# Keys and values of three quarters computed in the spare columns of the fourth query group

## The chip, the cores and the metric

The kernel runs on one core of one Trainium2 chip. The core has five engines that run side by side: TensorE (PE in the profile; its weight loads are PEld), VectorE (DVE), ScalarE (ACT), GpSimd (POOL) and SyncE (SP), which here only issues DMAs. The metric is the device time of one execution in microseconds, the median of several runs.

## The reference

A pre-normalized attention block with one shared key and value head, followed by a gated feed-forward block, on 2048 tokens of 448 features, all in float32:

```python
# S, D, H = 2048, 448, 16;  Dh = D // H = 28;  F = 1792
n = layernorm(x)
q = (n @ wq).reshape(B, S, H, Dh).transpose(0, 2, 1, 3)
k, v = n @ wk, n @ wv                      # one head of 28 for all 16 query heads
p = softmax(einsum("bhqd,bkd->bhqk", q, k) * Dh ** -0.5)
h = x + einsum("bhqk,bkd->bhqd", p, v).transpose(0, 2, 1, 3).reshape(B, S, H * Dh) @ wo
m = layernorm(h)
out = h + (silu(m @ w1) * (m @ w3)) @ w2
```

## The kernel before

The 2048 tokens are cut into four quarters t = 0 to 3 of 512 columns (X[t], transposed as XT[t]), the 16 heads into four groups g of four heads. A head has 28 features and lies in a band of 32 partitions, so a group fills 128 partitions and four of the 32 columns of each head's weights (WQ) are zeros. Every product with weights is made of float32 numbers split into a high and a low part: `mm_D` issues 11 matmuls, in two halves of 6 and 5.

The kernel has three parts: the front, a main loop over attention, and the feed-forward part. The change is in the front, with a tail of DMAs in the main loop. The front is an order written out by hand, the table FRONT. Each word is one step; every engine gets its instructions in the order of the words, and waits only for what an instruction needs:

- `tr.t.c`: four transposes of chunk c of quarter t (L223), and the copies to xh (ScalarE, L231) and xl (VectorE). `na`, `nm`: normalize on ScalarE, on VectorE; each is followed by a 64-column copy on GpSimd (L211). `st`: statistics on VectorE, with a power on GpSimd (L198).
- `wh`, `wp`, `wv`: split wq into high and low parts, on ScalarE, GpSimd, VectorE.
- `ka.t`, `kb.t`: the two halves of the key-value block of quarter t, 11 matmuls from WKV (wkvs). `kb` ends in the copies KH (ScalarE, L501) and vt (L503), and a DMA that doubles the 64 key rows to 128 (L504). `kl`: the low part KL on VectorE (L512), and its DMA. `va`: transposes of the values to VA.
- `kd.t`: the difference of the keys of two neighbouring quarters, on GpSimd (L507, tile kd).
- `qa.t.g`, `qb.t.g`: the two halves of the query block of quarter t and group g; `qb` ends in a copy to QR[t][:, g] (ScalarE, L534), or for group 0 of quarter 0 in the split queries qs. `qs.i`: the split of row i = 4t + g.
- `D.i.n.kp` and `U.i.n.kp`: quads, four matmuls of 32 partitions side by side (L277). A D takes scores against kd, and ScalarE applies a relu (L287); the U that follows takes them against KH, and VectorE adds both and reduces to the maximum (L291). `kp` is 0 for key quarters 0 and 1, and 1 for 2 and 3.
- `mx.0`: the row maxima of i = 0 (L307, L308) and four DMAs that put them into row 28 of qs (L314).

PSUM has eight banks of 512 columns. `bank()` deals them in the order in which `done()` gave them back, so that the table also settles which bank each step waits for.

The main loop makes 256 steps (row i, key chunk c of 128), two at a time; the units of the maxima run 20 steps ahead of it, the first 20 in the front. Work of other kinds is hung on steps by `at(step, ...)`: `max_done` and `max_out` (the max row of i, at 16i - 5 and 16i - 4), `o_norm` (DMAs sd and rb, L363 and L366), `build_qs`, and loads such as `load_w2`. What goes to SP's queue is issued strictly in that order, but as early as each DMA's own inputs allow.

Of the kernel before, what the change touches and what calls it, by code (L numbers as in the profile page):

```python
# [35 lines left out]
LAST_ORDER = ("1a 7c' 1b 4c' 6c' p0 0a 3a 1c 2a 5a 0b 2b 3b 2c 3c 5b 0c q "  # L36
              "6a 7a 5c 4a 4b 6b 7b").split()
FRONT = """
tr.0.1 tr.0.2 tr.0.3 wh.1 wh.0 ka.0 wp.0 wh.2 wp.1 st.1.1 kb.0 wh.3 wv.3 na.1.0 na.1.1 wv.2 qa.0.0
na.1.2 qa.0.1 na.1.3 st.2.1 qa.0.2 qb.0.0 qa.0.3 qb.0.2 qb.0.3 tr.1.0 tr.1.1 tr.1.2 tr.1.3 na.2.0  # L40
qb.0.1 ka.1 na.2.1 qs.2 na.2.2 kb.1 na.2.3 qa.1.0 kl.0 st.3 qa.1.2 tr.2.0 tr.2.1 tr.2.2 tr.2.3
qb.1.2 kd.1 nm.3.0 qb.1.0 nm.3.1 va.1 D.0.0.0 kl.1 qa.1.1 U.0.0.0 qb.1.1 nm.3.2 D.0.1.0 qa.1.3
nm.3.3 U.0.1.0 qb.1.3 D.0.2.0 qa.2.0 U.0.2.0 qs.1 va.0 tr.3.0 tr.3.1 tr.3.2 ka.2 tr.3.3 kb.2 kl.2
D.0.3.0 ka.3 kb.3 kl.3 kd.3 qb.2.0 U.0.3.0 qa.2.3 D.1.0.0 qb.2.3 U.1.0.0 qa.3.2 D.0.0.1 qb.3.2
U.0.0.1 qa.3.1 D.0.1.1 qb.3.1 U.0.1.1 qa.3.3 D.0.2.1 qb.3.3 U.0.2.1 qa.2.1 D.0.3.1 qb.2.1 U.0.3.1
mx.0 qa.3.0 va.3 D.1.0.1 qb.3.0 va.2 U.1.0.1 qa.2.2 qb.2.2
""".split()


# [1 line left out]
def block_kernel(  # L51
# [13 lines left out]
    ve, se, ge, pe, sy = nc.vector, nc.scalar, nc.gpsimd, nc.tensor, nc.sync  # L65
# [4 lines left out]
    def f(ap):  # L70
        return ap.bitcast(F32)
# [11 lines left out]
    ident = keep.tile([P, P], F32, name="ident")  # L83
# [3 lines left out]
    pexp, kb = small[:, :NQ], small[:64, NQ : NQ + 1]  # L87
# [3 lines left out]
    def slot(k, dt, name):  # L91
        return slots.tile([P, 2, T], dt, name=name, tag=f"slot{k}")
# [61 lines left out]
    def mm_D(ps, lhs, rhs, lsl, rsl, part=False, lows_last=False, half=None):  # L154


        terms = []
        for a, b in ((0, 0), (1, 0), (0, 1)):
            terms += [(a, c, b, c) for c in range(3)]
        terms += [(0, 3, 0, 3), (0, 3, 1, 3)][: 2 - part]  # L160
        if lows_last:
            terms.insert(6, terms.pop(9))
        for k, (a, ca, b, cb) in enumerate(terms):
            if half is None or half == (k > 5):
                pe.matmul(  # L165
                    ps, lhs[b][:, cb, lsl], rhs[a][:, ca, rsl],
                    start=(k == 0), stop=(k == len(terms) - 1 and not part),
                )
# [44 lines left out]
    XT = {}  # L213
# [35 lines left out]
    def build_qs(i, ps=None, spare=False):  # L249
        t, g = divmod(i, NG)  # L250
        QS[i] = slot(QSP[i % 3], F32R, "qs")
        MX[i] = MXS[i % 2]
        qh, ql = QS[i][:, 0], QS[i][:, 1]
        q = QR[t][:, g] if ps is None else ps
        if spare:
            ge.tensor_copy(qh, q)
        else:
            se.activation(qh, q, AF.Copy)
        (ge if ps is None else ve).tensor_tensor(ql, q, f(qh), op=ALU.subtract)
# [4 lines left out]
    def lane(j):  # L264
        return slice(32 * j, 32 * j + 32)
# [173 lines left out]
    def heat(n):  # L439
        for _ in range(n):  # L440
            pe.transpose(warm[:, :P], ident, ident)

    heat(34)
    ve.memset(VA, 1.0)
    ve.memset(f(NEG[0]), 0.0)
# [12 lines left out]

    def wq_low(eng, c):
        eng.tensor_tensor(WQ[1][:, c, :, :DH], wq4[:, c], f(WQ[0][:, c, :, :DH]), op=ALU.subtract)  # L460

    def load_wo():
        ge.memset(wo_r, 0.0)
        wov = wo.rearrange("(g j r) e -> j r g e", j=4, r=DH)
        for j in range(4):
            sy.dma_start(wo_r[32 * j : 32 * j + DH], wov[j])
# [24 lines left out]

    PP, VV = {}, {}

    def kv(half, t):
        if not half:
            PP[t] = bank()
        ps = PP[t]
        mm_D(ps[:96], WKV, XT[t], slice(0, 96), slice(0, T), half=half)
        if half:
            cols = slice(t * T, (t + 1) * T)  # L500
            se.activation(KH[0:64, cols], ps[0:64], AF.Identity, bias=kb)  # L501
            vt = VV[t] = VT[:, t % 2]
            se.activation(vt[64:96], ps[64:96], AF.Copy)  # L503
            sy.dma_start(f(KH[64:128, cols]), f(KH[0:64, cols]))  # L504

    def k_diff(t):
        ge.tensor_tensor(KD[:, t // 2], f(KH[:, t * T : (t + 1) * T]), f(KH[:, (t - 1) * T : t * T]),  # L507
                         op=ALU.subtract)

    def k_low(t):  # L510
        cols, ps = slice(t * T, (t + 1) * T), PP.pop(t)
        ve.scalar_tensor_tensor(KL[0:64, cols], ps[0:64], kb, f(KH[0:64, cols]), op0=ALU.add, op1=ALU.subtract)  # L512
        sy.dma_start(f(KL[64:128, cols]), f(KL[0:64, cols]))
        done(ps)

    def va(t):
        ps, vt = bank(), VV.pop(t)
        for n in range(NQ):
            pe.transpose(ps[:, 32 * n : 32 * n + 32], vt[64:96, n * P : (n + 1) * P], ident[64:96, 64:96])
        ve.tensor_copy(VA[:, NQ * t : NQ * t + NQ, :DH],  # L520
                       ps[:, :P].rearrange("p (n r) -> p n r", n=NQ)[:, :, :DH])
        done(ps)

    def q(half, t, g):
        if not half:
            PP[t, g] = bank()
        ps = PP[t, g]
        mm_D(ps, [w[:, :, 4 * g : 4 * g + 4].rearrange("p c h r -> p c (h r)") for w in WQ],
             XT[t], slice(0, P), slice(0, T), lows_last=True, half=half)
        if half:  # L530
            if t == g == 0:
                build_qs(0, ps)
            else:
                se.activation(QR[t][:, g], ps, AF.Copy)  # L534
            done(PP.pop((t, g)))

    def maxima(i):
# [3 lines left out]
    front = {  # L541
        "tr": ln_tr, "st": stats, "nm": ln_norm, "na": lambda t, n: ln_norm(t, n, se), "np": lambda t, n: ln_norm(t, n, ge),
        "wh": wq_high, "wp": lambda c: wq_low(ge, c), "wv": lambda c: wq_low(ve, c),
        "ka": lambda t: kv(False, t), "kb": lambda t: kv(True, t), "kl": k_low, "kd": k_diff, "va": va,
        "qa": lambda t, g: q(False, t, g), "qb": lambda t, g: q(True, t, g), "qs": build_qs,
        "D": lambda i, n, kp: quad(i, n, kp, True), "U": lambda i, n, kp: quad(i, n, kp, False), "mx": maxima,
    }
    ln_first()
    split_wkv()
# [22 lines left out]
    for i in range(NI - 1):  # L572
        e = NC * (i + 1)
# [3 lines left out]
    for t in range(NT - 1):  # L577
        e = NC * NG * (t + 1)
# [31 lines left out]
    for s in range(0, LAST, 2):  # L610
# [6 lines left out]
        for op in ORDER if us else LAST_ORDER:  # L617
# [19 lines left out]
            elif op[-1] != "'" or s != LAST - AHEAD:  # L637
                h = int(op[0])
# [64 lines left out]
    tl = NT - 1  # L703
# [83 lines left out]
```

## Time and profile before

| | us |
|---|---|
| median of 3 runs | 1180.38 (1180.21 to 1180.96) |
| the profiled execution | 1180.94 |
| its span in the trace | 1179.2 |
| first query matmul, in the span | 13.94 |
| first matmul of the main loop, in the span | 81.09 |
| first and last exponential of the main loop | 82.3 and 744.2 |

The granted clock is full in the whole span. In the rows of the timeline the first number is the start in us from the span's start, the second the length, then engine, line, operation, output and inputs, count, and in brackets the idle time before and what ended it. In a row of a table by stretch, the stretch is followed by its length, the busy time and count of PE, PEld, DVE, ACT and POOL, the clock, the DMA engines' busy share and GB/s. A row that begins with a line and has three durations gives the least, median and greatest in ns.

### The profile page before, as it was taken

To read this page: it belongs to the slowest core of one execution; us is meant where nothing else is said; L and a number is where in the kernel's file an instruction comes from. 1 tells how busy PE (TensorE), PEld (TensorE's weight loads), DVE (VectorE), ACT (ScalarE), POOL (GpSimd) and SP (SyncE) were. 2 spreads that over 40 slices of the span, in tenths; PEclk is the share of its full clock that TensorE was granted. 3 is DMA by queue.
4 is the path that set the end of the run, shared out by engine and by line. 5 is a ranking of instruction groups with operands and counts; after the bars stand their busy time and mean duration, and the time that the engine had idled before them with its cause. 6 is when DMAs were issued, how large, how long until landed. Compare 5 with 4: busy or idle time off the path is not lost. (4 is left out here: it accounts for less than half of the span.)

```text
span 1179.2 us, 24097 instructions
## 1 busy us (share of the span) xinstructions
PE 1167.5 (99%) x9585; PEld 726.4 (62%) x9585; DVE 810.8 (69%) x1478; ACT 730.9 (62%) x1389; POOL 330.2 (28%) x257
## 2 busy tenths in 40 slices
PE   9999999999999999999999999999999999999998
PEld 8654444445444445444445443688888888888887
DVE  7679999997889987999987972354454445444333
ACT  6769999996899996999986999411211111121111
POOL 4201101110110110111111032363555455455552
PEclk9999999999999999999999999999999999999999
DMA  4110101000010000010000010114000000000000
GB/s 165 32 29 2 35 16 33 12 11 2 11 45 4 11 11 2 11 47 11 3 11 11 3 46 11 42 44 118 1 32 1 1 1 32 1 1 32 1 1 32
DMA packets 32377, 26.92 MB, mean 23 GB/s; under 512 B 10824, under 2 KB 28936, under 8 KB 32264
## 3 DMA queue, kind: packets, MB, share of 16 engines
q1 hardware_dynamic: 31704, 25.32, 7.3%
q8 instruction: 75, 1.23, 0.4%
q14 instruction: 38, 0.31, 0.1%
q10 hardware_dynamic: 560, 0.06, 0.0%
HBM read 20.25 MB, written 3.80 MB: 20 GB/s over the span
## 5 line engine op out<-in xcount | busy, mean ns | idle before, releaser
L338 ACT ACTIVATE pt<-pb 128x512 f32<-128x512 f32 x1024 | 531.8, 611 | 11.6 <-PE pb L328 5.2
L283 DVE TENSOR_REDUCE mx<-pa 128x1 f32<-128x512 f32 x708 | 460.9, 684 | 52.7 <-PE pb L328 39.4
L328 PE MATMUL pb<-qs,KH 32*128 32x512 f32 x2048 | 342.7, 431 | 0.1
L277 PE MATMUL pa<-KH,qs 32*128 32x512 f32 x866 | 327.2, 488 | 0.0
L346 PE MATMUL po<-pt,VA 128*32 128x256 f32 (+1 forms) x2984 | 298.1, 471 | 5.8 <-ACT OT L350 5.4
L328 PE MATMUL pb<-qs,KL 32*128 32x512 f32 x1024 | 283.1, 419 | 0.0
L328 PEld LDWEIGHTS pb<-qs,KH 32*128 32x128 f32 x2048 | 174.6, 183 | 113.9 <-DVE mx L283 50.4
L165 PE MATMUL pa<-xh,w 128*128 128x512 f32 x784 | 202.1, 391 | 0.0
L675 ACT ACTIVATE rb<-pa 128x512 f32<-128x512 f32 x56 | 30.4, 596 | 250.5 <-PE pa L667 250.4
L165 PEld LDWEIGHTS pa<-xh,w 128*128 128x128 f32 x784 | 146.1, 188 | 30.4 <-issue 1.2
L277 PEld LDWEIGHTS pa<-KH,qs 32*128 32x128 f32 x866 | 142.3, 181 | 9.4 <-issue 2.5
L328 PEld LDWEIGHTS pb<-qs,KL 32*128 32x128 f32 x1024 | 136.6, 182 | 2.5
L692 PE MATMUL pb<-w2s,hid 128*128 128x448 f32 x648 | 136.9, 366 | 0.0
L346 PEld LDWEIGHTS po<-pt,VA 128*32 128x32 f32 x2984 | 58.8, 108 | 122.3 <-issue 105.0
L692 PEld LDWEIGHTS pb<-w2s,hid 128*128 128x128 f32 x648 | 119.4, 187 | 17.4 <-issue 9.8
L287 ACT ACTIVATE relu<-pa 128x512 f32<-128x512 f32 x158 | 91.2, 600 | 60.4 <-PE pa L277 50.1
L291 DVE CUSTOM_DVE_ANT_0 relu<-pa,relu 128x512 f32<-128x512 f32 x158 | 105.5, 682 | 9.0 <-PE pa L277 7.3
L392 POOL TENSOR_TENSOR w<-QR,w 128x1024 fp32r<-128x1024 f32 x32 | 84.0, 2640 | 92.9 <-PE pa L667 79.5
L684 DVE TENSOR_TENSOR hid<-rb,hid 128x512 fp32r<-128x512 f32 x56 | 72.6, 1296 | 39.2 <-ACT hid L683 39.2
L370 POOL TENSOR_TENSOR OT<-OT,rb 128x512 f32<-128x512 f32 x16 | 20.6, 1286 | 275.4 <-ACT pt L338 154.0
L165 PE MATMUL pa<-xl,w 128*128 128x512 f32 x336 | 94.5, 389 | 0.0
L391 DVE CAST w<-QR 128x1024 fp32r<-128x1024 f32 x32 | 22.4, 701 | 89.7 <-PE pa L165 77.3
(111 smaller groups left out, 962.3 us busy)
## 6 DMA issues: line engine op xcount, KB each, us to landing
rb<-sd SPq DMA_DIRECT2D x64, 64.0 KB
QR<-in_B_w_dram SPq DMA_DIRECT2D x16, 192.0 KB
X<-in_A_x_dram SPq DMA_DIRECT2D x3, 896.0 KB
out_dram<-X SPq DMA_DIRECT2D x3, 896.0 KB
w<-in_B_w_dram SPq DMA_DIRECT2D x8, 192.0 KB
w_wo<-in_B_w_dram SPq DMA_DIRECT2D x6, 224.0 KB
qs<-ngt SPq DMA_DIRECT2D x64, 2.0 KB
sm<-OT SPq DMA_DIRECT2D x64, 2.0 KB
```

The lines of the kernel that those rows point to most:

```text
L165: pe.matmul(ps, lhs[b][:, cb, lsl], rhs[a][:, ca, rsl], start=(k == 0), stop=(k == len(terms) - 1 and not part),)
L277: pe.matmul(self.ps, QS[i][r, 0, n * P : (n + 1) * P], ks[r], start=True, stop=True)
L283: ve.tensor_reduce(self.col(), self.ps, axis=AX.X, op=ALU.max)
L287: se.activation(r, self.ps, AF.Relu)
L291: ve.tensor_tensor_reduce(r, self.ps, r, 1.0, LOW, op0=ALU.add, op1=ALU.max, accum_out=self.col())
L328: pe.matmul(self.ps, (KH, KH, KL)[k][r, c * P : (c + 1) * P], QS[i][r, (0, 1, 0)[k]], start=(k == 0), stop=(k == 2))
L338: se.activation(pt, self.ps, AF.Exp, bias=0.0, scale=SCALE)
L346: pe.matmul(PO[i][32 * j : 32 * j + 32, q], VA[:, c], PT[i, c, j][:, q], start=(c == 0 and h0 == 0), stop=(c == NC - 1 and h1 == 2))
L392: ge.tensor_tensor(wl, W13[k], f(wh), op=ALU.subtract)
L675: se.activation(sg, ps[0], AF.Silu)
L684: ve.tensor_tensor(h[:, 1], sg, f(h[:, 0]), op=ALU.subtract)
L692: pe.matmul(Y[t][n][:, :D], hid[a][:, n * P : (n + 1) * P], w2s[:, b, :D], start=(k == 0 and m == 0), stop=(k == NF - 1 and m == 2))
```

## The change

For quarters 1 to 3 the key-value blocks are gone. The weights of group 3 are replaced by W3, whose 128 columns hold the key weights (band 0), the value weights (band 1) and heads 14 and 15 (bands 2 and 3). Heads 12 and 13, which had those bands, are cut into pieces of 12, 12 and 4 features (head 12) and 12, 8 and 8 (head 13): most go to the four unused columns of the heads of groups 0 to 2 (`wq_pads`, after the queries of quarter 0), the rest to unused columns of W3. GpSimd builds W3 with eight copies (`w3`) and the pads with eight more (`wd`). The key rows now come as 32, so that `dup` makes them 128 with three DMAs where one doubled 64. From step 18 of the main loop, `gather` collects heads 12 and 13 in rows 0 to 59 of QR[t][:, 3] with 16 DMAs a quarter, and clears the two rows that a later product must find zero. Four memsets on GpSimd are added at the start. The table FRONT is rewritten.

```diff
 FRONT = """
-tr.0.1 tr.0.2 tr.0.3 wh.1 wh.0 ka.0 wp.0 wh.2 wp.1 st.1.1 kb.0 wh.3 wv.3 na.1.0 na.1.1 wv.2 qa.0.0
...
+tr.0.1 tr.0.2 tr.0.3 wh.0 wh.1 wh.2 wp.0 wp.1 ka.0 st.1.1 wv.2 wh.3 wv.3 w3 kb.0 qa.0.1 na.1.0
...
+    W3 = slot(9, F32R, "w3")
...
+    ge.memset(f(W3.rearrange("p k (c j r) -> p k c j r", c=4, j=4)[:, :, :, 0, DH:]), 0.0)
+    for t in range(1, NT):
+        ge.memset(QR[t][0:64, 3], 0.0)
...
+    def w3_block():
+        for k in range(2):
+            w3 = W3[:, k].rearrange("p (c j r) -> p c j r", c=4, j=4)
+            ge.tensor_copy(w3[:, :, 0:2, :DH], WKV[k].rearrange("p c (j r) -> p c j r", r=32)[:, :, 0::2, :DH])
+            ge.tensor_copy(w3[:, :, 2:4, :DH], WQ[k][:, :, 14:16, :DH])
+            ge.tensor_copy(w3[:, :, 1, DH:], WQ[k][:, :, 12, 24:28])
+            ge.tensor_copy(w3[:, :, 2:4, DH:], WQ[k][:, :, 13, 20:28].rearrange("p c (j r) -> p c j r", j=2))
+
+    PADS = ((1, 12, 0, 0), (2, 12, 12, 0), (3, 13, 0, 0), (0, 13, 12, 1))
+
+    def wq_pads():
+        for k in range(2):
+            for e, h, d, g0 in PADS:
+                ge.tensor_copy(WQ[k][:, :, 4 * g0 : 12, DH + e], WQ[k][:, :, h, d : d + 12 - 4 * g0])
+
+    def gather(t, part):
+        q = QR[t]
+        if part < 4:
+            e, h, d, g0 = PADS[part]
+            r = 32 * (h - 12) + d
+            for g in range(g0, 3):
+                sy.dma_start(q[r + 4 * (g - g0) : r + 4 * (g - g0) + 4, 3], q[DH + e :: 32, g])
+        else:
+            for j in (2, 3):
+                sy.dma_start(q[44 + 4 * j : 48 + 4 * j, 3], q[32 * j + DH : 32 * j + 32, 3])
+            for g in (1, 2):
+                sy.dma_start(q[DH::32, g], q[DH:32, 3])
+            sy.dma_start(q[92::32, 3], q[DH : DH + 2, 3])
...
+    def dup(tl, n, cols):
+        for r in range(n, P, n):
+            sy.dma_start(f(tl[r : r + n, cols]), f(tl[0:n, cols]))
...
     def k_low(t):
-        cols, ps = slice(t * T, (t + 1) * T), PP.pop(t)
-        ve.scalar_tensor_tensor(KL[0:64, cols], ps[0:64], kb, f(KH[0:64, cols]), op0=ALU.add, op1=ALU.subtract)
-        sy.dma_start(f(KL[64:128, cols]), f(KL[0:64, cols]))
+        cols, ps, n = slice(t * T, (t + 1) * T), PP.pop(t), 32 if t else 64
+        ve.scalar_tensor_tensor(KL[0:n, cols], ps[0:n], kb[0:n], f(KH[0:n, cols]), op0=ALU.add, op1=ALU.subtract)
+        dup(KL, n, cols)
         done(ps)
...
-        mm_D(ps, [w[:, :, 4 * g : 4 * g + 4].rearrange("p c h r -> p c (h r)") for w in WQ],
-             XT[t], slice(0, P), slice(0, T), lows_last=True, half=half)
-        if half:
+        if t > 0 and g == 3:
+            ws = [W3[:, k].rearrange("p (c m) -> p c m", c=4) for k in range(2)]
+        else:
+            ws = [w[:, :, 4 * g : 4 * g + 4].rearrange("p c h r -> p c (h r)") for w in WQ]
+        mm_D(ps, ws, XT[t], slice(0, P), slice(0, T), lows_last=True, half=half)
+        if half and t > 0 and g == 3:
+            cols = slice(t * T, (t + 1) * T)
+            se.activation(KH[0:32, cols], ps[0:32], AF.Identity, bias=kb[0:32])
+            dup(KH, 32, cols)
+            vt = VV[t] = VT[:, t % 2]
+            se.activation(vt[32:64], ps[32:64], AF.Copy)
+            sy.dma_start(QR[t][24:28, 3], vt[60:64])
+            se.activation(QR[t][64:128, 3], ps[64:128], AF.Copy)
+            PP[t] = PP.pop((t, g))
+        elif half:
...
+    for t in range(1, NT):
+        for part in range(5):
+            at(13 + 5 * t + part, gather, t, part)
```

TensorE's rows below stand for whole steps: rows from wkvs are key-value blocks, from w_120 (W3) the new group 3, from OS_104 and OS_105 the other query blocks (high and low parts of WQ); kd is a D quad, KH a U quad, vt the transposes of `va`. First, TensorE around the keys of the last two quarters: before,

```order
L223 MATMUL pb<-ident,xn 128x128 x12
L165 MATMUL pb<-xh,wkvs 96x512 x3
L165 MATMUL pb<-xl,wkvs 96x512 x3
L223 MATMUL pb<-ident,xn 128x128 x4
L165 MATMUL pb<-xh,wkvs 96x512 x5
L277 MATMUL pa<-kd,qs 128x512 x4
L165 MATMUL pb<-xh,wkvs 96x512 x3
L165 MATMUL pb<-xl,wkvs 96x512 x3
L165 MATMUL pb<-xh,wkvs 96x512 x5
```

and in the changed kernel:

```order
L223 MATMUL pb<-ident,xn 128x128 x16
L165 MATMUL pb<-xh,w_120 128x512 x3
L165 MATMUL pb<-xl,w_120 128x512 x3
L277 MATMUL pa<-kd,qs 128x512 x4
L165 MATMUL pb<-xh,w_120 128x512 x5
L557 MATMUL pb<-ident,vt 128x32 x4
L277 MATMUL pa<-KH,qs 128x512 x4
L165 MATMUL pb<-xh,w_120 128x512 x3
L165 MATMUL pb<-xl,w_120 128x512 x3
L277 MATMUL pa<-kd,qs 128x512 x4
```

The two blocks of 11 matmuls that gave only keys and values are gone; the query blocks qa.2.3 and qa.3.3 stand in their place and are no longer among the later ones.

Second, TensorE where the quads of kp = 1 begin (U.1.0.0, then D.0.0.1 and U.0.0.1): before,

```order
L277 MATMUL pa<-KH,qs 128x512 x4
L165 MATMUL pb<-xh,OS_104 128x512 x3
L165 MATMUL pb<-xl,OS_104 128x512 x3
L277 MATMUL pa<-kd,qs 128x512 x4
L165 MATMUL pb<-xh,OS_104 128x512
L165 MATMUL pb<-xh,OS_105 128x512 x4
L277 MATMUL pa<-KH,qs 128x512 x4
```

and in the changed kernel:

```order
L277 MATMUL pa<-KH,qs 128x512 x4
L165 MATMUL pb<-xh,OS_104 128x512 x3
L165 MATMUL pb<-xl,OS_104 128x512 x3
L557 MATMUL pb<-ident,vt 128x32 x4
L277 MATMUL pa<-kd,qs 128x512 x4
L277 MATMUL pa<-KH,qs 128x512 x4
L165 MATMUL pb<-xh,OS_104 128x512
L165 MATMUL pb<-xh,OS_105 128x512 x4
```

The half query block between the D and the U is gone, and `va` has moved ahead of them; D.0.3.1, va.2 and U.0.3.1 stand together in the same way later.

Third, SP's queue in the main loop up to the max row of i = 2 (qs<-ngt): before, behind the DMAs rb of row 0,

```order
L366 DMA rb<-sd 32x512 x4
L180 DMA w2r_106<-in_B_w_dram 128x448
L180 DMA w2r_107<-in_B_w_dram 128x448
L180 DMA w2r_108<-in_B_w_dram 128x448
L314 DMA qs<-ngt_83 4x4x32 x4
```

and in the changed kernel the last part of the same stretch (QR_99 and QR_100 are quarters 2 and 3):

```order
L180 DMA w2r_106<-in_B_w_dram 128x448
L487 DMA QR_99<-QR_99 4x512 x3
L180 DMA w2r_107<-in_B_w_dram 128x448
L487 DMA QR_99<-QR_99 4x512 x2
L180 DMA w2r_108<-in_B_w_dram 128x448
L490 DMA QR_99<-QR_99 4x512 x2
L492 DMA QR_99<-QR_99 4x512 x2
L493 DMA QR_99<-QR_99 2x512
L487 DMA QR_100<-QR_100 4x512 x3
L314 DMA qs<-ngt_83 4x4x32 x4
```

Between rb and these rows stand 19 more gathers (13 of quarter 1, 6 of quarter 2), so that 32 DMAs have come between rb and the max row beside the three loads of w2.

More of the change, by code (lines that the diff above doesn't have):

```diff
@@ L38 @@
 FRONT = """
-tr.0.1 tr.0.2 tr.0.3 wh.1 wh.0 ka.0 wp.0 wh.2 wp.1 st.1.1 kb.0 wh.3 wv.3 na.1.0 na.1.1 wv.2 qa.0.0
[L40 to L46, printed above, removed]
+tr.0.1 tr.0.2 tr.0.3 wh.0 wh.1 wh.2 wp.0 wp.1 ka.0 st.1.1 wv.2 wh.3 wv.3 w3 kb.0 qa.0.1 na.1.0
+qa.0.0 na.1.1 qa.0.2 na.1.2 qa.0.3 na.1.3 st.2 kl.0 qb.0.0 qb.0.2 tr.1.0 tr.1.1 tr.1.2 tr.1.3 qb.0.1
+qa.1.3 qb.0.3 wd qb.1.3 nm.2.0 nm.2.1 nm.2.2 nm.2.3 st.3 kl.1 tr.2.0 qa.1.2 tr.2.1 kd.1 tr.2.2
+qb.1.2 tr.2.3 qa.1.0 va.0 D.0.0.0 nm.3.0 qb.1.0 qs.1 nm.3.1 nm.3.2 U.0.0.0 qa.1.1 D.0.1.0 qb.1.1
+nm.3.3 U.0.1.0 tr.3.0 tr.3.1 tr.3.2 tr.3.3 qa.2.3 D.0.2.0 qb.2.3 va.1 U.0.2.0 qa.3.3 D.0.3.0 qb.3.3
+kl.2 U.0.3.0 qa.2.2 D.1.0.0 qb.2.2 kl.3 U.1.0.0 qa.2.0 va.3 kd.3 D.0.0.1 U.0.0.1 qb.2.0 D.0.1.1
+qa.3.1 U.0.1.1 qb.3.1 D.0.2.1 qa.3.2 U.0.2.1 qb.3.2 D.0.3.1 va.2 U.0.3.1 mx.0 qs.2 qa.2.1 D.1.0.1
+qb.2.1 U.1.0.1 qa.3.0 qb.3.0
 """.split()
@@ L503, in kv @@
             se.activation(vt[64:96], ps[64:96], AF.Copy)
-            sy.dma_start(f(KH[64:128, cols]), f(KH[0:64, cols]))
+            dup(KH, 64, cols)
     def k_diff(t):
@@ L517, in va @@
         ps, vt = bank(), VV.pop(t)
+        r = lane(1 if t else 2)
         for n in range(NQ):
-            pe.transpose(ps[:, 32 * n : 32 * n + 32], vt[64:96, n * P : (n + 1) * P], ident[64:96, 64:96])
+            pe.transpose(ps[:, 32 * n : 32 * n + 32], vt[r, n * P : (n + 1) * P], ident[r, r])
         ve.tensor_copy(VA[:, NQ * t : NQ * t + NQ, :DH],
@@ L545, in block_kernel @@
         "qa": lambda t, g: q(False, t, g), "qb": lambda t, g: q(True, t, g), "qs": build_qs,
-        "D": lambda i, n, kp: quad(i, n, kp, True), "U": lambda i, n, kp: quad(i, n, kp, False), "mx": maxima,
+        "D": lambda i, n, kp: quad(i, n, kp, True), "U": lambda i, n, kp: quad(i, n, kp, False), "mx": maxima, "w3": w3_block, "wd": wq_pads,
     }
```

## Prediction

> **What bounds the kernel now.** I read the page's busy line first, then a table of engine busy time by stretch, then TensorE's own waits in the first 90 us, then the timeline of the front, which is the only part that the change writes anew.
>
> ```profile
> PE 1167.5 (99%) x9585; PEld 726.4 (62%) x9585; DVE 810.8 (69%) x1478; ACT 730.9 (62%) x1389; POOL 330.2 (28%) x257
> 13.94:81.09 67.15, 67.15 (x354) 46.64 (x352) 48.84 (x135) 46.71 (x86) 15.34 (x26) 1.00 0.11 32
> PE pb L441 <- POOL small L416: 1.3, 1, 1.3
> ```
>
> The second row is the stretch from the first matmul of the queries (13.94 us) to the first of the main loop (81.09 us): TensorE is busy in all 67.15 us at full clock, VectorE in 48.84, ScalarE in 46.71, GpSimd in 15.34. The third is the only wait of TensorE that the trace names up to 90 us, and it lies at the start. So the front is bounded by TensorE's own issue, and matmuls taken out there are worth their issue time until another engine's chain becomes late. Since busy time of pipelined matmuls is modelled, I price them by distances between starts:
>
> ```profile
> 13.94 0.85 PE L165 MATMUL pb<-xh,OS 128*128 128x512 f32 x3
> 17.36 0.84 PE L165 MATMUL pb<-xl,OS 128*128 128x512 f32 x3
> 25.70 0.85 PE L165 MATMUL pb<-xh,wkvs 128*96 128x512 f32 x3
> 28.26 0.85 PE L165 MATMUL pb<-xh,OS 128*128 128x512 f32 x3
> 54.48 0.51 PE L277 MATMUL pa<-KH,qs 32*128 32x512 f32 x4
> 54.92 0.95 PE L165 MATMUL pb<-xh,OS 128*128 128x512 f32 x3
> 56.50 0.50 PE L277 MATMUL pa<-kd,qs 32*128 32x512 f32 x4
> 56.93 1.43 PE L165 MATMUL pb<-xh,OS 128*128 128x512 f32 x5
> 58.29 0.51 PE L277 MATMUL pa<-KH,qs 32*128 32x512 f32 x4
> 75.66 0.25 PE L519 MATMUL pb<-ident,vt 32*128 32x32 f32 x1
> 76.34 1.44 PE L165 MATMUL pb<-xh,OS 128*128 128x512 f32 x5
> ```
>
> Rows one and two: 15 matmuls in 3.42 us, 0.228 each. Rows three and four: one whole key-value block (11 matmuls) is 2.56 us. Rows five to nine: a period of two quads (D, U) and one query block (11 matmuls) is 58.29 - 54.48 = 3.81 us; less 11 x 0.228 = 2.51, a quad between full-height matmuls costs 0.65: 0.22 to get in, 0.22 for its four parallel matmuls, 0.22 to get out. The last two rows: va and a quad together take 0.68 where a quad takes 0.44, so an adjacent va costs 0.24.
>
> **The change, part by part.**
>
> *Removed.* Three key-value blocks (quarters 2 to 4): 3 x 2.56 = 7.7 us of TensorE. On ScalarE nothing goes: KH, vt and QR of group 3 are still copied, the last with 64 rows at the same width. Four normalizations move from ScalarE to VectorE (nm.2 for na.2), about 2 us on an engine with 18 us free.
>
> *Order.* D.0.0.1 with U.0.0.1, and D.0.3.1 with va.2 and U.0.3.1, stand next to one another: each pair saves one way out and one way in, 2 x 0.44 = 0.9 us. TensorE's floor is therefore 8.6 us under before. Against it stand three waits, which I find by walking the new order with the row prices (query half 1.37 or 1.14 us, quad 0.65).
>
> *Wait 1, kd.3 (the difference of key quarters 3 and 2).*
>
> ```profile
> 53.53 0.68 ACT L501 ACTIVATE KH<-pb,small 64x512 fp32r<-64x512 f32 x1
> 54.24 0.46 SPq L504 DMA_DIRECT2D KH<-KH  x1
> 56.95 1.32 POOL L507 TENSOR_TENSOR kd<-KH 128x512 fp32r<-128x512 f32 x1 [9.41 <-DMA KH<-KH]
> 57.03 2.07 ACT L287 ACTIVATE relu<-pa 128x512 f32<-128x512 f32 x4 [1.58 <-PE pa L277]
> 58.93 0.69 DVE L291 CUSTOM_DVE_ANT_0 relu<-pa,relu 128x512 f32<-128x512 f32 x1 [0.89 <-PE pa L277]
> 59.55 0.69 DVE L291 CUSTOM_DVE_ANT_0 relu<-pa,relu 128x512 f32<-128x512 f32 x1
> 135.30 1.72 SPq L366 DMA_DIRECT2D rb<-sd  x4
> 138.97 1.28 POOL L370 TENSOR_TENSOR OT<-OT,rb 128x512 f32<-128x512 f32 x1 [16.40 <-ACT pt L338]
> ```
>
> From the start of the copy on ScalarE to the DMA is 0.71 us, from one DMA to kd 2.71, kd itself 1.32. Now three DMAs of 32 rows follow one another. The rb rows show four such DMAs, 0.43 apart, all landed 2.4 us after the last began; so the third costs 2 x 0.45 more, bounded by 0 and by 2 x 2.71. In the walk qb.3.3 ends at 49.7, but ScalarE is in the relus of D.0.3.0 until 50.8 (0.53 behind its quad, 0.52 each). KH.3 starts there, DMAs at 51.5, 52.0, 52.4, data at 54.9, kd.3 done at 56.2. TensorE reaches D.0.0.1 at 55.9 plus 0.2 for a bank of the relus of D.1.0.0. With a handover it waits 0.3 to 0.5. kd.1 in the same way: DMAs from 29.2, done near 34.1, wanted at 34.4: no wait, by 0.3 us.
>
> *Waits 2 and 3, PSUM banks of the adjacent quads.* The eight banks are dealt in the order in which they come free. One is held by the open query block and one went through va.3, so the fourth matmul of U.0.0.1 gets the bank that the first relu of D.0.0.1 leaves: 0.53 + 0.52 + 0.1 = 1.1 us after that quad started, where it would have come 0.22 after. That is 0.9 lost. U.0.3.1 gets the last two banks of U.0.2.1, whose reductions (first 0.64 behind its quad, 0.61 each) end 3.1 us after it started, so 1.3 after D.0.3.1 began (0.44 + 1.14 + 0.22 lie between); with va.2 it would have come 0.5 after. With the handover 0.9 is lost again, 1.8 together: the adjacency gives more back than it saves.
>
> *Loop start.*
>
> ```profile
> 73.62 0.51 PE L277 MATMUL pa<-KH,qs 32*128 32x512 f32 x4
> 76.83 0.22 DVE L307 TENSOR_REDUCE neg<-mx 128x16 fp32r<-128x64 f32 x1
> 77.36 2.44 SPq L314 DMA_DIRECT2D qs<-ngt  x4
> 81.09 0.50 PE L277 MATMUL pa<-KH,qs 32*128 32x512 f32 x1
> 81.38 0.46 PE L328 MATMUL pb<-qs,KH 32*128 32x512 f32 x1
> ```
>
> From U.0.3.1 (73.62) to the max row's DMAs is 3.74 us and from these to the first score matmul (81.38) 4.02, which bounds how long the four DMAs take. After U.0.3.1 the new order has two query blocks and two quads, 6.3 us and a 0.2 way in, against 7.47 before: it lacks two va. Since U.0.3.1 waits as above, its DMAs go out near 71.6, and the score matmul can follow by 75.6; TensorE arrives at 75.5 to 75.8. Wait at most 0.1. The six KL copies ahead of them on SP go out behind kl.3, by 57.
>
> *Sum.* -7.7 - 0.9 + 0.4 (kd.3) + 0.3 (single banks of the relus around U.1.0.0) + 1.8 (waits 2, 3) + 0.1 = -6.0; the walk itself, with a few hundredths at each handover, sets the loop's start at 75.5 against 81.09, -5.6. I take -5.7.
>
> *Costed at nothing: GpSimd.*
>
> ```profile
> 58.20 1.60 POOL L463 MEMSET OT<- 128x1792 f32 x1
> 4.66 0.57 POOL L198 TENSOR_TENSOR rs<-rs,small 128x1 f32<-128x1 f32 x1 [2.93 <-DVE rs L197]
> 18.22 0.25 POOL L201 TENSOR_SCALAR rs<-rs 128x4 f32<-128x4 f32 x1
> L256 POOL CAST qs<-QR 128x512 fp32r<-128x512 f32 x13 | 7.9, 611 | 246.7 <-PE pb L328 246.7
> L211 POOL COPY xn<-xn 128x64 f32<-128x64 f32 x32 | 9.2, 297 | 16.6 <-DVE xn L209 6.5 <-ACT xn L207 6.5 <-PE pb L519 2.4
> ```
>
> The new memsets (three of 512 columns, 1.60 x 512/1792 = 0.46 each, one small) lie in the 2.93 us before 4.66. The eight copies of w3 have 16 to 224 elements: between 0.2 and 0.4 by the last two rows, 2.3 us together, or 4.9 if each took the whole 0.61. They start at 18.5 and stand ahead of the xn copies that tr.1.3 wants at 23.1: free up to about 3.6 us (4 x 0.27 for the xn copies behind them), 1.3 lost at the upper end. The lower end is taken, as the sizes lie around the 64-column row. The eight pad copies (48 elements) start behind qb.0.3's first matmul at 26.3, 0.25 each, done by 28.4; qa.1.2 wants the first four at 28.8 and qb.1.2 the rest at 31.1.
>
> *Costed at nothing: the 48 gather DMAs on SP's queue.* They run in the main loop, where the groups that they complete are built from step 49 on. But SP issues in order, and the max row of unit row i = 2 stands behind 32 of them.
>
> ```profile
> L504 SPq DMA_DIRECT2D KH<-KH x4: 461/475/509, 14.9 to 54.2; - x4
> L366 SPq DMA_DIRECT2D rb<-sd x64: 307/413/1653, 135.3 to 766.4; - x64
> L355 SPq DMA_DIRECT2D sm<-OT x64: 513/588/1706, 125.7 to 748.7; - x64
> 137.07 1.37 SPq L180 DMA_DIRECT2D w2r<-in_B_w_dram  x3
> 151.67 2.34 SPq L314 DMA_DIRECT2D qs<-ngt  x4
> 161.18 0.50 PE L328 MATMUL pb<-qs,KH 32*128 32x512 f32 x1
> ```
>
> In times of before: SP is free at 138.44 (after the w2 rows), and issues the max row at 151.67, which TensorE reads at 161.18. With 4.02 us to land, it may go out as late as 157.2. Ahead of it come 32 gathers at c each and, twice, about 1.2 us in which the last of a quarter's gathers waits for two issued 0.9 and 1.4 before it (2.4 us to land, as above). 138.44 + 2.4 + 32 c reaches 157.2 at c = 0.51. By the rb row (0.41) it goes out at 154.0, by the KH row (0.475) at 156.0, by the sm row (0.59) at 159.7, 2.5 too late. A gather is four whole rows of 2 KB, nearest to rb and KH: no loss, with 1 to 3 us in hand.
>
> The profiled execution took 1180.94 us with a span of 1179.2, 0.56 above the median of the runs, 1180.38. 1180.94 - 5.7 = 1175.2 for its like, 1174.7 for the median.
>
> **The rivals.**
>
> *The floor.* Banks and kd.3 come in time because the walk is late by some tenths everywhere: 8.6 saved. Then the max row bounds the loop's start (3.74 + 4.02 from U.0.3.1, where TensorE needs 6.5), which gives 1.2 back: 7.4, 1173.0. Against it: the bank chains follow from single rows of the trace and do not shift with the walk.
>
> *Front or queue stalls more.* The w3 copies at their upper end (1.3), gathers at the sm row's price (2.5), or kd.3 later by another 1.5: saving 2 to 4.4, so 1176 to 1178.4, 1177 in the middle.
>
> *The split copy of the keys lands one after the other.* If each of the three DMAs took 2.71 by itself, kd.1 would be done at 29.2 + 8.1 + 1.3 = 38.6, 4.2 late, and kd.3 at 51.5 + 9.4 = 60.9, 4.8 after the walk's 56.1: 9.0 against a gain of 5.7 in which 0.4 of it is counted, 2.9 slower, 1183.3; half of it would end in no difference. The four rb DMAs speak against it. The Trainium skill, DMA: Bandwidth & Descriptors, Rules for kernel authors, advises joining small transfers into a large one, since under 64 KB one pays mostly overhead; by the fixed part of about 2.0 us in its section Anatomy of one DMA, paid one at a time, three copies would be an estimated 6 us. The rb rows, four DMAs landed within 3.7 us of the first issue, do not bear out that it is paid one at a time.
>
> *Slower: SP's queue.* Should a gather hold SP for 0.77 us or more, the max row goes out at 165.5 or later, 8.2 late, TensorE stands that long once, and the gain of 5.7 is lost with 2.5 on top: 1183. It decides from c = 0.69 on. No group of small DMAs in the rows has such a median, though single ones reach 1.7.
>
> **How the numbers follow.** Two results nearer than 0.2% (2.4 us) count as no change. Walk as taken, 1173.7 to 1175.9: 0.58. Floor: 0.14. More stalls: 0.20, of which 0.05 ends within 0.2%. Keys one after the other: 0.04, half of it no change. SP slower: 0.04, of which 0.01 stops short at no change. Faster 0.58 + 0.14 + 0.15 = 0.87, same 0.05 + 0.02 + 0.01 = 0.08, slower 0.05. The range 1172.7 to 1177.6 takes in the floor and most of the third case.
>
> **What the profile after would show.** Right: no matmul from wkvs beyond the first 11; the first score matmul near 75.7; TensorE's named waits in the front at the adjacent quads and at kd.3, some 2 to 3 us; the period of two quads and a query block still 3.8. Wrong: a wait of tr.1.3 on GpSimd; D.0.0.0 after 34.6; a pause of score matmuls near 155 (161.18 - 5.7) with the max row's DMAs just ahead; main-loop periods that differ from before, for which I see no ground.

## The result and the profile after

| | before | after |
|---|---|---|
| median of 4 runs each, on the same chip, us | 1180.34 (1180.21 to 1180.96) | 1174.22 (1174.13 to 1174.64) |
| ratio | | 0.9945, 95% interval 0.9933 to 0.9956 |
| the profiled execution, its span | 1180.94, 1179.2 | 1174.14, 1172.0 |
| first query matmul, in the span | 13.94 | 13.88 |
| first score matmul of the main loop | 81.38 | 74.56 |

The change made the kernel 6.1 us faster, 0.55%. Where it came from is read first from the busy line of the page after, the stretch from the first query matmul to the main loop, and the first matmuls of the loop:

```profile
PE 1159.4 (99%) x9552; PEld 720.2 (61%) x9552; DVE 812.2 (69%) x1482; ACT 728.1 (62%) x1385; POOL 334.0 (29%) x275
13.88:74.55 60.67, 60.36 (x321) 42.18 (x319) 50.54 (x139) 43.62 (x82) 18.08 (x40) 1.00 0.15 43
74.55 0.49 PE L277 MATMUL pa<-KH,qs 32*128 32x512 f32 x1
74.56 0.50 PE L328 MATMUL pb<-qs,KH 32*128 32x512 f32 x1
```

33 matmuls fewer on TensorE, 9585 to 9552, are the three key-value blocks. The stretch is 60.67 us where it was 67.15: 6.48 of the gain lie there, at full clock. TensorE is still busy in nearly all of it, so the front stays bounded by TensorE's issue. From the loop's start on nothing is gained or lost: the loop's copies (L350) run 6.5 to 6.9 us ahead of before all the way. The rows at the four places of the prediction:

```profile
32.46 1.32 POOL L544 TENSOR_TENSOR kd<-KH 128x512 fp32r<-128x512 f32 x1 [0.87 <-DMA KH<-KH]
33.94 0.50 PE L277 MATMUL pa<-kd,qs 32*128 32x512 f32 x2
34.60 1.43 PE L165 MATMUL pb<-xh,OS 128*128 128x512 f32 x5
50.13 0.66 ACT L573 ACTIVATE KH<-pb,small 32x512 fp32r<-32x512 f32 x1
50.82 1.78 SPq L529 DMA_DIRECT2D KH<-KH  x3
54.16 1.32 POOL L544 TENSOR_TENSOR kd<-KH 128x512 fp32r<-128x512 f32 x1 [14.21 <-ACT relu L287]
55.27 0.43 PE L557 MATMUL pb<-ident,vt 32*128 32x32 f32 x4
55.53 0.61 PE L277 MATMUL pa<-kd,qs 32*128 32x512 f32 x4
55.88 1.38 PE L277 MATMUL pa<-KH,qs 32*128 32x512 f32 x4
56.49 0.44 PEld L277 LDWEIGHTS pa<-KH,qs 32*128 32x128 f32 x3 [0.43 <-DVE mx L291]
57.18 1.42 PE L165 MATMUL pb<-xh,OS 128*128 128x512 f32 x5
66.20 0.51 PE L277 MATMUL pa<-kd,qs 32*128 32x512 f32 x4
66.55 0.37 PE L557 MATMUL pb<-ident,vt 32*128 32x32 f32 x4
67.00 1.12 PE L277 MATMUL pa<-KH,qs 32*128 32x512 f32 x4
67.61 0.19 PEld L277 LDWEIGHTS pa<-KH,qs 32*128 32x128 f32 x3 [0.43 <-DVE mx L291]
68.05 0.96 PE L165 MATMUL pb<-xh,OS 128*128 128x512 f32 x3
70.75 2.32 SPq L314 DMA_DIRECT2D qs<-ngt  x4
```

The first three rows are kd.1, done at 33.78, D.0.0.0 right behind it and the query block that follows. The next five are the chain of kd.3: the copy, three DMAs that take SP 0.6 us each, the difference 3.34 us after the first of them began, va.3, and D.0.0.1 at the end of kd.3 (55.48). The row of kd.3 names a relu that ended just before it, but kd.3 reads keys alone; kd.1, whose row names the DMAs, began 3.42 us after its first DMA (29.04 to 32.46), and in two_queues below the row of kd.3 names the DMAs as well, so they end this wait too.

Then wait 2: from D.0.0.1 to the next query block 1.65 us pass, where two quads without a wait take 0.22 for each quad's matmuls and 0.22 to get out, 0.66; about 1.0 is lost. It stands inside the group of four matmuls of 1.38 us, so the list of TensorE's waits names none after the first 14 us. The weight loads (PEld) of the same matmuls do name it: the second matmul of U.0.0.1 waits 0.43 us for VectorE's last reduction of U.1.0.0. The last two go at 56.68 and 56.78, behind VectorE's copy of va.3, which ends at 56.62, and the first relu of D.0.0.1, which ends at 56.66. The prediction named the relu alone; it does come last, but only 0.04 us behind VectorE.

Wait 3 is the same at D.0.3.1, va.2 and U.0.3.1: 1.85 where 0.9 would do, 0.95 lost, and its weight loads name VectorE's reductions (of U.0.2.1, the last of them done at 67.56). Last the max row: its DMAs go out at 70.75, and the first score matmul follows 3.81 later. The period of two quads and a query block is 3.82 (from the D at 58.54 to the D at 62.36), as before.

### The profile page after: what moved, and what is told of

It reads as the page before. It is cut to its first block, busy times and chain, and to the rows that moved or that the text cites. A ratio compares the mean times of both kernels' runs of the same rounds, so it can differ in the third digit from the quotient of the medians.

```text
span 1172.0 us, 24130 instructions
## 1 busy us (share of the span) xinstructions
PE 1159.4 (99%) x9552; PEld 720.2 (61%) x9552; DVE 812.2 (69%) x1482; ACT 728.1 (62%) x1385; POOL 334.0 (29%) x275
```

## The experiments

Each is compared with runs of the kernel before on the same chip, and its diff is against the changed kernel. Expectations count from the changed kernel's 1174.2, which was measured on a chip where the kernel before takes 1180.34. On the chips of the experiments it takes 1180.61 (kv_back to no_gather, and all_ahead), 1180.80 (keys_late, filler, two_queues) and 1180.78 (eight_ahead, six_ahead). "Chip for chip" below therefore stands for 6.12, the gain of the change, less the distance to before on the same chip.

The loop's start in a single trace is good to about half a us: four kernels whose front is that of the changed kernel have their first score matmul at 74.63 (no_gather), 74.93 (all_ahead), 75.00 (eight_ahead) and 74.50 (six_ahead), where the changed kernel has 74.56.

### The matmuls put back (kv_back)

```diff
-qa.1.3 qb.0.3 wd qb.1.3 nm.2.0 ...
+qa.1.3 qb.0.3 wd qb.1.3 xk.1 nm.2.0 ...
...
+    def kv_unread(t):
+        ps = bank()
+        mm_D(ps[:96], WKV, XT[t], slice(0, 96), slice(0, T))
+        done(ps)
```

Three blocks of 11 matmuls, one behind each of qb.1.3, qb.2.3 and qb.3.3, into a bank that nobody reads.

> The changed kernel with the three key-value blocks of 11 matmuls put back behind qb.1.3, qb.2.3 and qb.3.3, into a bank that nobody reads. If the gain is TensorE's issue time of these matmuls, the time rises by 3 x 2.5 = 7.6 us, less 0.2 where TensorE waits for kd.3 anyway: 1181.6 (1181.0 to 1182.0), above the kernel before. If the gain came from the new order or from other engines, the blocks fill waits and the time stays under 1179.

Measured 1181.97 (1181.69 to 1182.17), ratio 1.0011 [1.0002, 1.0020]. The first score matmul comes at 82.22, 7.66 later than in the changed kernel; the term was 7.68. Chip for chip the time is 7.5 us above the changed kernel. So the removed matmuls are all of the gain: the rest of the change, with the matmuls in, costs 0.8 us at the loop's start (82.22 against 81.38).

### The merged blocks in the order of before (old_order)

```diff
-... qb.2.2 kl.3 U.1.0.0 qa.2.0 va.3 kd.3 D.0.0.1 U.0.0.1 qb.2.0 D.0.1.1 ...
+... qb.3.3 kl.3 kd.3 qb.2.0 U.0.3.0 D.1.0.0 U.1.0.0 qa.3.2 D.0.0.1 qb.3.2 ...
```

FRONT is that of before, without the blocks that are gone and with w3 and wd put in.

> The merged blocks in the order of before: qa.t.3 and qb.t.3 stand where ka.t and kb.t stood and their old places are dropped, w3 and wd are put in. The same 33 matmuls are gone. Theory: three quads now stand together at three places (D.0.1.0 to D.0.2.0, U.0.3.0 to U.1.0.0, U.0.1.1 to U.0.2.1) and wait for banks, relus and VectorE's 2.45 us a quad, so only about a third to a half of the 7.7 us is kept: 1177 (1175.5 to 1178.5). Rival: the order does not matter and only the matmuls count: 1173 to 1174.5.

Measured 1183.22 (1182.27 to 1186.36), ratio 1.0030 [1.0018, 1.0042]: slower than before, a miss by 6 us. The timeline of TensorE at two of the places where three quads now stand together (in this kernel L270 is the quads, L158 the query matmuls), and two stretches of its table:

```profile
39.59 1.60 PE L270 MATMUL pa<-KH,qs 32*128 32x512 f32 x4
40.71 1.75 PE L270 MATMUL pa<-kd,qs 32*128 32x512 f32 x4
42.38 0.98 PE L158 MATMUL pb<-xh,OS 128*128 128x512 f32 x3
55.21 0.39 PE L270 MATMUL pa<-kd,qs 32*128 32x512 f32 x2
57.26 0.50 PE L270 MATMUL pa<-kd,qs 32*128 32x512 f32 x2 [1.65 <-DVE KL L542]
57.87 2.32 PE L270 MATMUL pa<-KH,qs 32*128 32x512 f32 x4
42.00:46.00 4.00, 4.00 (x17) 2.64 (x18) 2.55 (x9) 2.91 (x5) 0.78 (x1) 0.67 0.00 0
46.00:50.00 4.00, 4.00 (x25) 3.59 (x24) 3.90 (x12) 2.14 (x4) 0.50 (x1) 0.90 0.00 0
58.00:62.00 4.00, 3.64 (x9) 2.14 (x10) 4.00 (x13) 2.29 (x4) 2.67 (x2) 0.81 0.28 69
62.00:66.00 4.00, 4.00 (x18) 2.11 (x18) 0.48 (x3) 2.47 (x5) 0.15 (x1) 0.77 0.00 0
```

Three quads in a row ask for twelve banks where there are eight: from the U at 39.59 to the query block at 42.38 pass 2.8 us, where two quads take 0.66, and from the D at 55.21 to the block at 60.12 pass 4.9. The 1.65 us in there are a wait for the low part of the keys (KL) on VectorE, which still holds the bank of the last key block. In the new order query blocks lie between most of these quads, and the banks come back in that time. And TensorE's granted clock, full everywhere in before and after, falls behind both places: 0.33 x 4 + 0.10 x 4 = 1.7 us of lost clock, then 0.19 x 4 + 0.23 x 4 = 1.7 again. Of the 9.1 us by which the first score matmul (83.62) is later than in the changed kernel, 3.4 are the clock and the other 5.7 are left for waits; I had expected 2.8, all waits. So the merge paid in the order that keeps the quads apart, and not in this one.

### The gathers left out (no_gather)

```diff
-    for t in range(1, NT):
-        for part in range(5):
-            at(13 + 5 * t + part, gather, t, part)
```

Heads 12 and 13 of quarters 1 to 3 are then incomplete.

> The changed kernel without the 48 gather DMAs (heads 12 and 13 of quarters 1 to 3 stay incomplete). Theory: SP's 48 issues and their traffic are hidden, 1174.2 within 0.4. Rival: they cost the main loop something, 1173.5 or less.

Measured 1174.08 (1173.33 to 1174.43), ratio 0.9945 [0.9932, 0.9957]. Its span, 1172.3 in the median, is that of the changed kernel, 1172.1: the 48 DMAs are hidden, as they were costed. Chip for chip the time is 0.4 below, and this lies outside the span (see why the prediction was right).

### More gathers ahead of the max row (all_ahead, eight_ahead, six_ahead)

```diff
-            at(13 + 5 * t + part, gather, t, part)
+            at(min(13 + 5 * t + part, 27), gather, t, part)
```

Thirteen DMAs more go to SP ahead of the max row of i = 2.

> The gathers of quarter 3 are hung on step 27 at the latest, so that 13 more DMAs stand ahead of the max row of i = 2 on SP's queue. The trace of the changed kernel has that row issued at 149.4 and read near 154.6. Theory (SP issues in order, 0.55 us a gather, one wait of 1 us): issued at 157.5, landed 2.5 to 4 us later, TensorE stands 5.5 to 7 us once: 1179.7 to 1181.2. Rival: nobody waits there, 1174.2; or the slack is larger than read, 1175 to 1178.

Measured 1182.0 (1181.04 to 1183.61), ratio 1.0013 [1.0004, 1.0022]. First SP's queue in the changed kernel, then in this one, with TensorE's first score matmul behind the row and three stretches of the table:

```profile
126.64 2.75 SPq L366 DMA_DIRECT2D rb<-sd  x4
149.37 2.29 SPq L314 DMA_DIRECT2D qs<-ngt  x4
```

```profile
148.26 5.96 SPq L487 DMA_DIRECT2D QR<-QR  x11
157.45 2.28 SPq L314 DMA_DIRECT2D qs<-ngt  x4
161.03 0.76 PE L328 MATMUL pb<-qs,KH 32*128 32x512 f32 x1 [5.49 <-DMA qs<-ngt]
161.00:163.00 2.00, 1.97 (x14) 1.11 (x18) 0.97 (x2) 0.26 (x1) 0.00 (x0) 0.50 0.00 0
163.00:165.00 2.00, 2.00 (x19) 0.84 (x11) 0.92 (x2) 1.24 (x3) 0.00 (x0) 0.50 0.00 0
165.00:167.00 2.00, 2.00 (x25) 0.76 (x26) 1.24 (x3) 1.87 (x5) 0.00 (x0) 0.80 0.00 0
```

A gather takes SP 0.54 to 0.55 us. The stall is there, 5.5 us on the row's DMAs, and the score matmul starts 3.58 after the first of the four went out, so the changed kernel, which reads the row at 154.69, had 1.74 us in hand. But behind the pause the clock is 0.50 for some 4 us, which costs 2 x 0.50 + 2 x 0.50 + 2 x 0.20 = 2.4 more. That is why it was slower than expected: 5.5 and 2.4 are 7.9, and chip for chip it is 7.5 above the changed kernel. Two more kernels cut the pause, to see from which length on the clock falls; eight_ahead moves eight of the thirteen, six_ahead six (with `part < 3` in the same line):

```diff
-            at(13 + 5 * t + part, gather, t, part)
+            at(min(13 + 5 * t + part, 27 if part < 4 else 32), gather, t, part)
```

> Eight of the last quarter's gathers move ahead of the max row of i = 2. Eleven gathers in one run took 5.96 us with all thirteen ahead, 0.54 each, so the row's four DMAs go out 4.3 us later, near 153.7; there the first score matmul started 3.58 us after the first of the four, so it starts near 157.3 where the changed kernel has 154.69: TensorE stands 2.6 us. Theory A (a pause that fills most of some 3 to 4 us halves the granted clock for as long again, as with all thirteen ahead, where the clock was 0.50 from 161 to 165): some 2 us more are lost, and the time is 1174.2 + 4.6 = 1178.8 (1178.2 to 1179.4), with the clock near 0.5 in the 3 us behind the pause. Theory B (the pause alone counts, and the low clock came from its 5.5 us): 1176.8 (1176.4 to 1177.3), the clock at 1.00.

> As before with six gathers ahead: the max row 3.25 us later, TensorE stands 1.5 us at the max row. Theory A with a limit near half of the 3 to 4 us (in the kernel with late keys, pauses of 1.1 and 0.35 us within 2 us were followed by a clock of 0.50 for 2 us, in the profiled run but by its granted clock not in every run): the runs part into some near 1175.7 with a clock of 1.000 and some near 1177.5 with 0.998. Theory B: all near 1175.7 (1175.3 to 1176.2). If there is more in hand ahead of the read than 1.7 us, 1174.2 to 1175.

eight_ahead: 1176.7 (1176.23 to 1177.52), ratio 0.9964 [0.9950, 0.9977]. six_ahead: 1175.78 (1174.89 to 1177.28), ratio 0.9957 [0.9944, 0.9969]. First the rows of eight_ahead, its profiled execution the one of 1177.52, then those of six_ahead, the one of 1175.78:

```profile
157.04 0.47 PE L328 MATMUL pb<-qs,KH 32*128 32x512 f32 x1 [1.44 <-DMA qs<-ngt]
157.00:159.00 2.00, 1.96 (x22) 1.21 (x26) 1.29 (x2) 0.93 (x2) 0.00 (x0) 0.86 0.00 0
159.00:161.00 2.00, 2.00 (x19) 0.64 (x15) 1.38 (x2) 1.56 (x4) 0.00 (x0) 0.50 0.00 0
161.00:163.00 2.00, 2.00 (x22) 0.93 (x18) 1.00 (x2) 1.84 (x4) 0.00 (x0) 0.78 0.00 0
```

```profile
156.18 0.47 PE L328 MATMUL pb<-qs,KH 32*128 32x512 f32 x1 [1.09 <-DMA qs<-ngt]
157.00:159.00 2.00, 2.00 (x29) 0.92 (x27) 1.79 (x4) 1.76 (x4) 0.00 (x0) 1.00 0.00 0
```

The pauses are 1.44 and 1.09, shorter than my 2.6 and 1.5, since TensorE had matmuls left that do not need the row. After 1.44 the clock halves in the profiled execution and 2 x (0.14 + 0.50 + 0.22) = 1.7 us go, together 3.2; this execution is 2.9 above the changed kernel chip for chip. After 1.09 the clock stays at 1.00, and the median of six_ahead is 1.1 above, the pause alone. By their own granted clocks the five runs of six_ahead part into four of 1.000 (1174.89 to 1175.99) and one of 0.998 (1177.28), whose pause no trace shows.

Neither theory came out as it stood. The clock of 0.50 behind 1.44 us is what theory A said and theory B denied. But the median of eight_ahead, 1176.7, lies below A's range and in B's, which was worked out for a pause of 2.6; and its two runs of 1176.23 are 1.6 above the changed kernel chip for chip, which leaves no room for 1.7 us of clock. So a pause of 1.44 us can halve the clock, and does not in every run.

### The keys later (keys_late)

```diff
+            junk = dr_pool.tile([96, T], F32, name="junk", bufs=3)
+            for r in range(0, 96, 32):
+                sy.dma_start(junk[r : r + 32], f(KH[0:32, cols]))
```

Three more DMAs stand on SP ahead of the three copies of each quarter's keys.

> The changed kernel with three more DMAs (the same 32 key rows to DRAM) issued ahead of the three key copies of each quarter, 0.59 us each. Theory: kd.1 and kd.3 come just in time (in the trace of the changed kernel their ends lie 0.1 us ahead of D.0.0.0 and of D.0.0.1), so both are 1.7 later and TensorE stands for both: plus 3.3, 1177.5 (1176.8 to 1178.2). Rival: one of them has slack, plus 1.6; or both, 1174.2.

Measured 1176.88 (1175.90 to 1179.53), ratio 0.9970 [0.9961, 0.9979], chip for chip 2.2 above the changed kernel. The profiled execution took 1179.1 (its front was 0.9 late before the first key copy of quarter 1):

```profile
36.08 0.51 PE L277 MATMUL pa<-kd,qs 32*128 32x512 f32 x4 [0.80 <-POOL kd L544]
58.73 0.60 PE L277 MATMUL pa<-kd,qs 32*128 32x512 f32 x4 [1.14 <-POOL kd L544]
59.91 0.49 PE L277 MATMUL pa<-KH,qs 32*128 32x512 f32 x1 [0.35 <-ACT relu L287]
```

TensorE now waits for both differences, by name. The three new DMAs take SP 1.29 and 1.25 us, 0.43 each and not 0.59. Counted from va.0 and va.3, the matmuls ahead of the two quads, kd.1 and kd.3 are each done 1.3 later than in the changed kernel, and the two quads start 1.2 and 1.3 later. So the differences had 0.1 us in hand or nothing, as the theory said, and its 3.3 was too much by the price of a DMA. In this execution the two pauses at kd.3, together 1.5 us, again halve the clock (the table is in the last section). The runs with a mean clock of 1.000 lie between 1175.90 and 1177.01, those under it between 1177.8 and 1179.53.

### Work put into wait 2 (filler)

```diff
-... va.3 kd.3 D.0.0.1 U.0.0.1 qb.2.0 ...
+... va.3 kd.3 D.0.0.1 xq.2.0 U.0.0.1 qb.2.0 ...
```

xq issues five more matmuls, low by low parts, into the open query block.

> Five more full-height matmuls (low part times low part, added to the open block q.2.0) between D.0.0.1 and U.0.0.1, 1.14 us and one more way out and in, 0.44: 1.6 us of TensorE. Theory: U.0.0.1 waits there about 1.0 us for the bank of D.0.0.1's first relu, and the filler covers it: plus 0.6, 1174.8. Rival: the stretch is TensorE's own time, plus 1.6, 1175.8.

Measured 1175.18 (1174.94 to 1175.50), ratio 0.9955 [0.9942, 0.9967]; chip for chip 0.5 above the changed kernel, where 0.6 was expected and the rival said 1.6. Five matmuls at 0.228 and a way out and in, 0.44, are 1.58 us. From D.0.0.1 to the block behind U.0.0.1 pass 2.34 us (55.53 to 57.87) where 1.65 did, 0.69 more, so 0.9 of the 1.58 were hidden in the wait. That bounds wait 2 from below, and agrees with the 1.0 read from the rows.

### One key copy on ScalarE's queue (two_queues)

```diff
-            sy.dma_start(f(tl[r : r + n, cols]), f(tl[0:n, cols]))
+            eng = se if tl is KH and n == 32 and r == 64 else sy
+            eng.dma_start(f(tl[r : r + n, cols]), f(tl[0:n, cols]))
```

> The middle one of the three key copies is issued by ScalarE, so that the last one goes out 0.6 us earlier. Theory: kd.3 costs TensorE at most 0.15 us in the changed kernel, so 1174.1 within 0.3; D.0.0.1 0.1 earlier in the trace. Rival, the 0.3 to 0.5 us that the prediction put on this wait: 1173.7 to 1173.9. If ScalarE's issue delays its relus, slower by some tenths.

Measured 1175.5 (1174.88 to 1176.37), ratio 0.9958 [0.9945, 0.9970]: chip for chip 0.8 us above the changed kernel, and 0.8 at the loop's start (75.33), where I expected no difference.

```profile
51.27 0.52 ACTq L530 DMA_DIRECT2D KH<-KH  x1
53.67 1.04 PE L277 MATMUL pa<-KH,qs 32*128 32x512 f32 x4
54.21 0.18 PEld L277 LDWEIGHTS pa<-KH,qs 32*128 32x128 f32 x1 [0.30 <-ACT relu L287]
53.98 1.31 POOL L545 TENSOR_TENSOR kd<-KH 128x512 fp32r<-128x512 f32 x1 [13.88 <-DMA KH<-KH]
```

The issue holds ScalarE for 0.5 us, so its copies and relus return their banks later, and U.1.0.0, the quad at 53.67, takes 1.04 where it takes 0.5: the weight load of its last matmul waits for a relu by name. The chain from the key copy to kd.3 did get shorter, 3.40 where it was 4.03, but the copy itself starts 0.45 later, so kd.3 begins only 0.18 earlier. The banks round U.1.0.0 come just in time in the changed kernel, and 0.6 us more on ScalarE is enough to make TensorE wait for them.

## Why the prediction was right

The forecast was 1174.7, the time 1174.22. The mechanism was right: a front bounded by TensorE's issue gives back the matmuls taken out, less what the adjacent quads wait. Step by step, at the loop's start:

| term | predicted | the rows show |
|---|---|---|
| three key-value blocks | -7.7 | -7.66 (kv_back) |
| ways out and in at the adjacent quads | -0.9 | not measured apart; waits 2 and 3 below are counted against times without them |
| wait 1, kd.3 | +0.4 | about +0.15: U.0.0.1 starts 0.61 after va.3; va.0 and D.0.0.0 took 0.67 (33.93 to 34.60) with a way out of 0.22, so 0.45 would do |
| single banks round U.1.0.0 | +0.3 | 0 |
| wait 2, wait 3 | +0.9, +0.9 | +1.0, +0.95 |
| max row and handovers | +0.5 | about 0, what is left of the 6.5 |
| sum | -5.6 | -6.5 |

So the banks were sized well, though the profile shows them another way than the prediction said: it expected named waits of TensorE at the adjacent quads and at kd.3, and only the weight loads name those at the quads. The rival of the floor, in which the banks come in time, is out by the same rows. And the terms that were too high were those reached by adding many row prices: the walk ran some tenths late (55.9 for D.0.0.1 where it started at 55.53), and each handover had a few hundredths too many. The key copies were a mis-sized part that did not show: SP takes 0.6 for each of three, not 0.45, but kd.3 began 2.14 us after the last of them did, not 2.4, and the chain from the first DMA to kd.3 was 3.34 us against 3.4 in the walk. That the three land one after the other, the rival with 1183.3, would have made this 8.1. The fixed part of about 2.0 us that stood beside it (the Trainium skill, DMA: Bandwidth & Descriptors, Anatomy of one DMA, where it is fitted to DMAs issued by GpSimd) is not paid one DMA after the other here: three of them took these 3.34 us.

The front gave 6.5 and the time only 6.1. The difference lies outside the span: the runs' time less their span was 1.79 us in the runs of before and 2.14 in those of the changed kernel, while the span itself fell by 6.5 (1180.34 less 1.79 is 1178.55, and the changed kernel's median is 1172.1). no_gather, all_ahead and old_order have 1.8 there, the others 2.1. What makes these 0.35 us stays open. It brought the time nearer to the forecast than the sum of the front deserved, which is luck.

Of what was costed at nothing, GpSimd held: its rows of the w3 copies and pads are

```profile
18.32 0.36 POOL L469 CAST w<-wkvs 128x224 fp32r<-128x224 f32 x1
20.03 0.20 POOL L472 CAST w<-OS 128x32 fp32r<-128x32 f32 x1
24.73 0.74 POOL L479 CAST OS<-OS 128x48 fp32r<-128x48 f32 x4 [0.18 <-PE pb L165]
```

1.9 us for the eight copies where 2.3 was taken, and the pads done by 25.5 where 28.4 was. The gathers held too, but by another margin than worked out. My step put the limit at 0.51 us a gather and took 0.41 to 0.475; they take 0.55, which by that step should have stalled. The limit was wrong, in three terms. The last rb was out at 129.4, 1.0 us earlier than its 137.0 less the 6.6 of the front. The two waits inside the queue, taken at 1.2 each, came to 0.9 with all other gaps: from 129.47 to 149.37 pass 19.9 us, of which 32 gathers are 17.7 and the three loads of w2 1.3. And the row needs 3.58, not 4.02. 1.74 us were in hand, as all_ahead shows, out of the 1 to 3 that I gave; by the price that I took for a gather this was luck.

The rival of more stalls did not come, but the kernel is near it: six more gathers (1.1), one DMA of each quarter's keys on another engine (0.8) or three more on SP's queue (2.2) cost, chip for chip, 0.8 to 2.2 us each.

## What to carry to other kernels

Where one engine is bound by its own issue through a whole stage, matmuls taken out there are worth their start-to-start distance; but count the waits that the new neighbours make, for the removed work was also the time in which banks came back: the same merge in the old order was slower than before. Look for these waits in the rows of the weight loads too, where the list of TensorE's waits has none. Hunt for waits that stand within some 3 us of each other, since beyond their own length they can cost the clock. And before a DMA is moved to an idle queue, look at what the issuing engine has to hand back in that half microsecond.

## What had not been expected of the hardware

In the profiled executions of eight_ahead and keys_late a TensorE pause of 1.44 us, or two of 1.14 and 0.35 within 2.3 us, was followed by a granted clock of one half. The table of keys_late by stretch:

```profile
58.00:60.00 2.00, 0.93 (x8) 0.60 (x8) 0.62 (x4) 0.74 (x2) 0.67 (x1) 1.00 0.44 108
60.00:62.00 2.00, 2.00 (x6) 1.09 (x6) 2.00 (x7) 1.32 (x3) 0.00 (x0) 0.78 0.28 68
62.00:64.00 2.00, 2.00 (x8) 1.23 (x8) 0.42 (x2) 1.63 (x4) 0.00 (x0) 0.50 0.00 0
64.00:66.00 2.00, 2.00 (x11) 1.21 (x10) 0.16 (x1) 1.03 (x3) 0.00 (x0) 0.87 0.00 0
```

2 x (0.22 + 0.50 + 0.13) = 1.7 us of clock are lost, which is 3.4 us at half speed; eight_ahead lost 1.7, old_order 1.7 at each of two places, where TensorE had lost 2.1 and 4.2 us to banks. So at these four places one fall cost 1.7 us, whatever the pause was. Behind the 5.5 us of all_ahead it cost 2.4; but there the clock fell while TensorE still stood, 0.99 from 157 to 159 us and 0.50 from 159 to 161, so that half speed lasted 6.8 us in all, twice 3.4.

No single length decides it. A pause of 1.09 us left the clock at full in the profiled run of six_ahead, and by the mean clock in three of its other four; 1.44 us in eight_ahead did not cost it in every run; and the changed kernel's own waits of 1.0 and 0.95 us, 11 us apart, left it at 1.00. That runs of one kernel part into two groups some 2 us apart, as in six_ahead and keys_late, fits a limit that depends on where the pause falls in a window, but no run here shows the window itself. The Trainium skill, TensorE: Matmul & The Clock Gate, Part 1: The HAM clock gate, says that the clock is either half or full and is judged by a window of about 3.4 us that runs freely; the 3.4 us agree. It names an idle window as the condition of the fall; in eight_ahead and keys_late TensorE was idle for less than half of one. How much of a window has to stand idle was not measured.
